# A linear-attention and rational-FFN kernel: another order in its front, chunk 7 by split products, three casts by transfers

## The chip, the cores and the metric

The kernel runs on one core of a Trainium2 chip. The metric is the device time of one launch in microseconds (us), here the median of three runs. A profiled execution has its own time, which is given beside its span (first to last instruction in the trace). Engines: PE (TensorE, matmuls), ACT (ScalarE), DVE (VectorE), POOL (GpSimd), SP (SyncE, which issues most transfers).

## The reference

```
kv  = einsum('bhsd,bhse->bhde', k, v)            # 8 batches, 8 heads, 576 tokens, 64 wide
out = einsum('bhsd,bhde->bhse', q, kv)
x   = out / sqrt(mean(out*out, -1) + 1e-6) * g_norm       # -> 4608 tokens x 512
h   = x @ w_in                                            # 512 x 2048
P   = a0 + a1*h + a2*h^2 + a3*h^3
Q   = 1 + |b0|*|h| + |b1|*h^2
y   = (P / (Q + 1e-6)) @ w_out                            # 2048 x 512
```

The weights come as 64-bit floats and are converted to 32 bits on the chip.

## The kernel before, in words

Tokens go in nine tiles (t) of 512. In each tile the hidden width goes in 16 chunks (c) of 128. One pair (t, c) is a slot; slots run in order (i = 16 t + c). A slot evaluates the rational function of one h (128 x 512 in PSUM) on ACT and DVE (`ew_a` to `ew_d`); PE meanwhile makes the h of the next slot (`gemm1`) and adds the slot two back to the output sums (`gemm2`, tiles `acc`), and it does the attention of the next tile: `kvp` (k times v, from the transferred `kvm`), `op` (kv times q, from `qr`), `ms` (mean squares). All engines follow the order of the code.

Products have two forms. *f32*: one matmul call on 32-bit floats, which the trace shows as two matmuls. *Split*: each operand is a high part (a cast to float32r) and a low part (the rest); three matmuls (high x low, low x high, high x high). Tile 0 uses f32 for `gemm2`, and for `gemm1` of chunks c < `EARLY` (8); later chunks of tile 0 and all other tiles are split. So split parts of tile 0's x and of the weights are needed from chunk 8 on, in `x[0]` and `whl`.

Weights come in units of two chunks, ("wi", c) of w_in and ("wo", c) of w_out. `fetch_w` loads the raw 64-bit words; `signed` (ACT), `lowbits` (ACT or DVE), `conv_b1` and `conv_add` (DVE) make 32-bit floats of them; `split_w` makes the high part with a cast on ACT, and `low_by_transfer`, in the next slot, writes the negated high part on POOL and then issues a transfer from POOL that adds the original on top of it (an accumulating transfer). A dependency puts that negation beside the slot's `q`. `split_x0` does the same for tile 0's x, in two groups of 512 KB. The table `schedule` gives for each unit the slot of the fetch (None and -1: in the front), of the conversion, of the split, and the tags of the SBUF cells for raw words, floats and split parts.

The front (lines 671 to 733) makes tile 0's attention in two halves of 256 tokens: `first_kv`; `first_o(p, k)` for pair p of heads and half k (`op`, half 0 reads `first_qa`, half 1 `first_qb`); `first_squares`; `first_ms` (32 small matmuls); `first_newton` (reciprocal root r: three steps on ACT, two on DVE); `first_rb` (32 small matmuls that spread r); `first_norm` (DVE, four of them, which finish x0). Beside that, unit u0 = ("wi", 0) is converted chunk by chunk (`one`, `two`), then u1 = ("wi", 2) and u2 = ("wo", 0). h of chunks 0 and 1 is made in halves, first half 0 of both, then half 1.

Transfers from SP run through one queue, in the order of their issue; those from POOL through another, on the same 16 transfer engines.

Of the kernel before, what the change touches and what calls it, by code (L numbers as in the profile page):

```python
# [23 lines left out]
def linear_attention_then_rational_ffn(  # L24
# [106 lines left out]
    def f32(t):  # L131
# [3 lines left out]


    schedule = {
# [16 lines left out]
    }  # L154
    units = list(schedule)

# [8 lines left out]
    for c in range(4, NF, 2):  # L165
        made[schedule["wi", c][1] + 1].append(("wi", c, None))

    EARLY = 8
    ON_VECTOR = (("wi", 6),)

    def unsplit(t, c):
# [7 lines left out]
    def fetch_w(u, halves=(slice(0, 2),)):  # L179
        kind, c = u  # L180
        if u not in raws:
            raws[u] = wpool.tile([P, 2 * DM], I64, tag=schedule[u][3], name=f"raw_{kind}{c}")
        src = w_in[c:c + 2].rearrange("c p k f -> p c (k f)") if kind == "wi" else \
            w_out[c:c + 2].rearrange("c p f -> p c f")
        to = raws[u].rearrange("p (c f) -> p c f", c=2)
        for js in halves:
            nc.sync.dma_start(to[:, js], src[:, js])
# [40 lines left out]
    def split_w(u):  # L228
        kind, c = u
        w = ups.pop(u)  # L230
        cells = schedule[u][5]
        if isinstance(cells, str):
            hl = wpool.tile([P, 2, 2 * DM], F32R, tag=cells, name=f"{kind}hl{c}")
            wh, wl = hl[:, 0], hl[:, 1]
        else:
            wh, wl = (wpool.tile([P, 2 * DM], F32R, tag=g, name=f"{kind}{n}{c}") for g, n in zip(cells, "hl"))
        for j in range(2):
            js = slice(j * DM, (j + 1) * DM)
            whl[kind, c + j] = wh[:, js], wl[:, js]
        ACT.copy(wh, w)  # L240
        lows.append((wl, wh, w))

    lows = []
# [6 lines left out]
    def split_x0(g):  # L250
        pool, tag = ((xpool, "xA"), (wpool, "e"))[g]
        xt = pool.tile([P, 2, 2, TW], F32R, tag=tag, name=f"x_0_{g}")
        of = x0[:, 2 * g:2 * g + 2]
        ACT.copy(xt[:, :, 0], of)
        x.setdefault(0, []).extend((xt[:, p, 0], xt[:, p, 1]) for p in range(2))
        lows.append((xt[:, :, 1], xt[:, :, 0], of))

# [373 lines left out]
    def first_o(p, k):  # L631
        q = (qa0, tq0[:, 4 * P:])[k][:, p * HW:(p + 1) * HW]
        PE.matmul(o0[p][k], kvf[:, 0, p], q, start=True, stop=True)

    def first_squares(g, k, made=0):
        for p in range(2 * g + made, 2 * g + 2):
            first_o(p, k)
        for p in range(2 * g, 2 * g + 2):
            ACT.activation(sq0[p][:, halves[k]], o0[p][k], AF.Square)

# [9 lines left out]
    def first_newton(k):  # L650
        cs = slice(k * BW, (k + 1) * BW)
        return newton_rstd(ms0[:, cs], r0[:, cs], r2[:, cs])
# [3 lines left out]
    def first_rb(k):  # L656
        rb0[:] = [oo[p % 2][p // 2][:, 0] for p in range(NPAIR)]
        if k == 0:
            for p, (pool, tag, bufs) in ((1, (ps_at, "at", 1)), (3, (ps_h, "h", 2))):
                rb0[p] = pool.tile([P, TW], F32, tag=tag, name=f"rb_0_{p}", bufs=bufs)[:, 0:HW]  # L660
        for b in range(NBLK):
            for p in range(NPAIR):
                ps = slice(p * Q4, (p + 1) * Q4)
                PE.matmul(rb0[p][:, b * BW:(b + 1) * BW], spread[ps, b], r0[ps, k * BW:(k + 1) * BW], start=True, stop=True)
# [4 lines left out]
            DVE.scalar_tensor_tensor(xp, xp, ghalf, rb0[p], ALU.mult, ALU.mult)  # L669

    u0, u1, u2 = units[:3]
    fetch_w(u0, (one_chunk,))
    nc.sync.dma_start(tq0[:, 4 * P:], of_qb)
    fetch_w(u0, (next_chunk,))
    fetch_w(u1, (one_chunk, next_chunk))
    fetch_w(u2)
    ctx.enter_context(tc.manual_schedule())
# [3 lines left out]
    for p in range(NPAIR):  # L681
        first_kv(p)
        if p < NPAIR - 1:
            warm(1, idle)
    for g in range(2):
        first_squares(g, 0)
        for p in range(2 * g, 2 * g + 2):
            DVE.tensor_copy(x0[:, p, halves[0]], o0[p][0])
# [5 lines left out]
        fetch_w(u)  # L694
    ms0 = ps_at.tile([P, TW], F32, tag="ms", name="ms_0", bufs=1)
    first_ms(0)
    signed(u0, one)
    lowbits(u0, one, "V")
    conv_b1(u0, one)
    newton = first_newton(0)  # L700
    newton()
    conv_add(u0, one)
    first_squares(0, 1)
    signed(u0, two)
    first_o(2, 1)
    first_rb(0)
    first_squares(1, 1, 1)
    lowbits(u0, two)
    first_norm(0)
    h0 = [h_room(0, c) for c in range(2)]  # L710
    gemm1_part(0, 0, h0[0], halves[0], range(0, 2), halves[0])
    first_ms(1)
    gemm1_part(0, 0, h0[0], halves[0], range(2, NPAIR), halves[0])
    conv_b1(u0, two)
    conv_add(u0, two)
    newton = first_newton(1)
    newton()
    for p in range(NPAIR):
        ACT.copy(x0[:, p, halves[1]], o0[p][1])
    ACT.activation(b1abs, abg[:, 5:6], AF.Abs)  # L720
    gemm1_part(0, 1, h0[1], halves[0], range(0, 2), halves[0])
    first_rb(1)
    gemm1_part(0, 1, h0[1], halves[0], range(2, NPAIR), halves[0])
    lowbits(u1, both, "V")
    first_norm(1)
    for c in range(2):
        gemm1_part(0, c, h0[c], halves[1], on=halves[1])
    signed(u1)
    conv_b1(u1, both)
    conv_add(u1, one)  # L730
# [8 lines left out]
    for i, (t, c) in enumerate(slots[:-1]):  # L739
# [17 lines left out]
                evacuate(slots[i - LAG][0])  # L757
        for u in at_slot(2, i):
            split_w(u)
        if i in (1, 3):  # L760
            split_x0(i // 3)
        if i == 0:
            ph = h0[1]
        elif i in (1, 3):
# [78 lines left out]
```

## Time and profile before

| | |
|---|---|
| median of 3 runs | 885.57 us (885.53 to 885.66) |
| profiled execution, own time | 885.92 us |
| its span | 884.2 us |
| PE, DVE, ACT, POOL busy | 876.4, 765.6, 690.1, 87.0 us |
| moved by transfers | 75.10 MB, of it 64.63 by SP's queue, 9.44 by POOL's |

Busy time is that in which an engine has an instruction in work. Matmuls overlap and their ends are modelled, so durations of PE's rows add up to more than the time they take; the distance of two starts is the safer reading. A small wait in square brackets names what ended it.

### The profile page before, as it was taken

The page shows a single profiled execution, that of the slowest core. Times are in us where ns is not written, and L with a number is a line of the kernel's source. Part 1 is how long each engine was busy: PE and PEld are TensorE (multiplying, and loading weights), DVE is VectorE, ACT ScalarE, POOL GpSimd, SP SyncE. Part 2 cuts the span into 40 slices and gives each one's busy share as a digit, 9 for nine tenths or more (in the row PEclk, how much of TensorE's full clock was granted, in tenths as well). Part 3 has the DMA queues.
Part 4 walks back from the last instruction along what each step waited for, and adds up shares of the span by engine and source line. Part 5 has one row for each costly group of instructions (what it writes and reads, how often), then busy time and mean ns, then how long its engine had stood idle before and what let it go on. Part 6 is the DMA issues. An engine that isn't in the chain of part 4 may idle for free.

```text
span 884.2 us, 12008 instructions
## 1 busy us (share of the span) xinstructions
PE 876.4 (99%) x4432; PEld 688.8 (78%) x4432; DVE 765.6 (87%) x1225; ACT 690.1 (78%) x1167; POOL 87.0 (10%) x88
## 2 busy tenths in 40 slices
PE   8999999999999999999999999999999999999998
PEld 6545657878887888888887888788878887888886
DVE  3988898879987998889888997799879988898887
ACT  4999979887877788777877787768767886777665
POOL 3254436422000000000000000000000000000000
PEclk9999999999999999999999999999999999999999
DMA  9987338544122203130223022221002020201001
GB/s 365 393 265 226 72 72 215 140 111 96 60 84 72 49 12 125 35 93 1 72 84 101 8 71 73 73 49 57 27 13 50 9 66 10 49 1 48 0 1 49
DMA packets 26811, 75.10 MB, mean 85 GB/s; under 512 B 2624, under 2 KB 2624, under 8 KB 26752
## 3 DMA queue, kind: packets, MB, share of 16 engines
q1 hardware_dynamic: 23760, 64.63, 21.4%
q0 software_dynamic: 2848, 9.44, 5.9%
q8 instruction: 35, 0.57, 0.3%
q10 hardware_dynamic: 144, 0.26, 0.1%
q14 instruction: 24, 0.20, 0.1%
HBM read 55.32 MB, written 9.57 MB: 73 GB/s over the span
## 4 chain that ended last, share of the span: by engine, by line
PE 94%; DVE 3%; DMA 2%; ACT 1%; issue 0%
PE h L485 14%; PE h L486 13%; PE h L487 13%; PE acc L553 12%; PE acc L555 12%; PE acc L554 12%; PE acc L544 6%; PE h L481 3%; PE kvp L330 2%; DMA first_qb<-in_first_dram 2%; PE ms L404 1%; PE op L387 1%; PE op L388 1%; PE op L386 1%; DVE gl L532 1%; PE op L382 0%
## 5 line engine op out<-in xcount | busy, mean ns | idle before, releaser
L495 ACT ACTIVATE d<-h 128x512 f32<-128x512 f32 x143 | 85.7, 599 | 146.2 <-PE h L487 145.2
L497 DVE SCALAR_TENSOR_TENSOR q<-d,b1abs,q 128x512 f32<-128x512 f32 x143 | 107.1, 749 | 90.6 <-ACT q L496 90.4
L485 PE MATMUL h<-x,wihl 128*128 128x512 f32 (+1 forms) x420 | 167.0, 398 | 0.0
L486 PE MATMUL h<-x,wihl 128*128 128x512 f32 (+1 forms) x420 | 162.8, 388 | 0.0
L487 PE MATMUL h<-x,wihl 128*128 128x512 f32 (+1 forms) x420 | 162.7, 387 | 0.0
L553 PE MATMUL acc<-woh,gl 128*128 128x512 f32 x316 | 123.1, 389 | 0.1
L554 PE MATMUL acc<-wol,gh 128*128 128x512 f32 x316 | 123.0, 389 | 0.0
L555 PE MATMUL acc<-woh,gh 128*128 128x512 f32 x316 | 122.9, 389 | 0.0
L508 ACT ACTIVATE d<-q,bias 128x512 f32<-128x512 f32 x143 | 105.3, 736 | 15.8 <-DVE q L497 15.0
L498 ACT ACTIVATE u<-h,na 128x512 f32<-128x512 f32 x143 | 111.9, 783 | 0.0
L509 ACT ACTIVATE d<-d,bias 128x512 f32<-128x512 f32 x143 | 103.6, 725 | 4.7
L505 DVE SCALAR_TENSOR_TENSOR u<-u,na,h 128x512 f32<-128x512 f32 x143 | 106.1, 742 | 0.6
L515 DVE SCALAR_TENSOR_TENSOR u<-u,na,d 128x512 f32<-128x512 f32 x143 | 106.6, 746 | 0.0
L513 DVE SCALAR_TENSOR_TENSOR q<-q,d 128x512 f32<-128x512 f32 x143 | 98.4, 688 | 0.2 <-ACT d L509 0.2
L499 DVE TENSOR_TENSOR u<-u,h 128x512 f32<-128x512 f32 x143 | 97.8, 684 | 0.4
L496 ACT ACTIVATE q<-h,abg 128x512 f32<-128x512 f32 x143 | 97.9, 685 | 0.0
L485 PEld LDWEIGHTS h<-x,wihl 128*128 128x128 f32 x420 | 78.9, 188 | 23.6 <-DVE q L513 4.2
L486 PEld LDWEIGHTS h<-x,wihl 128*128 128x128 f32 x420 | 78.9, 188 | 16.8 <-issue 1.6
L487 PEld LDWEIGHTS h<-x,wihl 128*128 128x128 f32 x420 | 78.9, 188 | 16.5
L532 DVE TENSOR_TENSOR gl<-u,gh 128x512 fp32r<-128x512 f32 x127 | 90.7, 714 | 0.0
L521 DVE SCALAR_TENSOR_TENSOR u<-q,u 128x512 f32<-128x512 f32 x127 | 87.4, 689 | 2.4
L531 ACT CAST gh<-u 128x512 fp32r<-128x512 f32 x127 | 79.9, 629 | 3.5 <-DVE u L521 3.3
(162 smaller groups left out, 1448.3 us busy)
## 6 DMA issues: line engine op xcount, KB each, us to landing
kvm<-in_kv_dram SPq DMA_DIRECT2D x28, 640.0 KB
raw_wo<-in_w_out_dram SPq DMA_DIRECT2D x8, 1024.0 KB
qr<-in_qT_dram SPq DMA_DIRECT2D x32, 256.0 KB
out_dram<-ob SPq DMA_DIRECT2D x16, 512.0 KB
rb<-rd SPq DMA_DIRECT2D x28, 256.0 KB
raw_wi<-in_w_in_dram SPq DMA_DIRECT2D x6, 1024.0 KB
wihl<-wiw POOLq DMA_DIRECT2D x6, 512.0 KB, 4.5
wol<-wow POOLq DMA_DIRECT2D x5, 512.0 KB, 6.9
```

Source lines behind the costliest of these rows:

```text
L485: PE.matmul(ph, wh, xl, start=(kc == 0), stop=False)
L486: PE.matmul(ph, wl, xh, start=False, stop=False)
L487: PE.matmul(ph, wh, xh, start=False, stop=(kc == NPAIR - 1))
L497: q_made = DVE.scalar_tensor_tensor(q, d, b1abs, q, ALU.mult, ALU.add)
L498: ACT.activation(u, ph, AF.Identity, bias=na[:, 2:3], scale=na[:, 3:4])
L505: DVE.scalar_tensor_tensor(u, u, na[:, 1:2], ph, ALU.add, ALU.mult)
L508: ACT.activation(d, q, AF.Ln, bias=bias[:, 2:3], scale=QSC)
L509: ACT.activation(d, d, AF.Exp, bias=bias[:, 3:4], scale=-1.0)
L515: DVE.scalar_tensor_tensor(u, u, na[:, 0:1], d, ALU.add, ALU.mult)
L553: PE.matmul(o, gl[:, ss], wh, start=(c == 0), stop=False)
L554: PE.matmul(o, gh[:, ss], wl, start=False, stop=False)
L555: PE.matmul(o, gh[:, ss], wh, start=False, stop=(c == NF - 1))
```

## The change

- Front, transfers: `first_qb` is issued ahead of both chunks of u0, where it stood between them.
- Front, order: all four `first_o` of half 1 run directly behind `first_ms(0)`, where they stood in two pieces behind the first conversion. Newton of half 0 comes ahead of u0's conversion; `first_ms(1)` ahead of h_0's first half, which is no longer cut in two; the copies of x (ACT) ahead of `first_newton(1)`; `first_rb(1)` ahead of h_1's first half; the low bits of u1 behind `first_norm(1)`.
- `EARLY` is 7: h of chunk 7 in tile 0 is made by split products. For this ("wi", 6) is split in slot 3, where it was split in slot 17, and its low part follows in slot 4.
- The high parts of tile 0's x (both groups, slot 0; before, slots 1 and 3) and of ("wi", 6) are made by transfers from POOL that convert on the way, where ACT cast them. The low parts of x follow in slots 2 and 3 (before, 2 and 4).
- The table: other cells for split parts, and later fetches of four units.

```diff
     schedule = {
-        ("wi", 0): (None, None, 11, "g0", "f0", "g3"),
-        ("wi", 2): (None, None, 13, "g1", "f1", "g5"),
+        ("wi", 0): (None, None, 11, "g0", "f0", ("f4", "f6")),
+        ("wi", 2): (None, None, 13, "g1", "f1", ("f8", "f10")),
...
-        ("wi", 6): (-1, 1, 17, "g4", "f4", ("f10", "f12")),
+        ("wi", 6): (-1, 1, 3, "g4", "f4", "g4"),
...
-        ("wi", 14): (3, 8, 10, "g4", "f12", "g4"),
-        ("wo", 10): (4, 9, 23, "g5", "f13", ("f5", "f4")),
-        ("wo", 12): (6, 11, 25, "g7", "f14", ("f7", "f9")),
-        ("wo", 14): (8, 13, 27, "g1", "f15", ("f11", "f13")),
+        ("wi", 14): (4, 8, 10, "g5", "f12", "g5"),
+        ("wo", 10): (6, 9, 23, "g7", "f13", ("f3", "f5")),
+        ("wo", 12): (8, 11, 25, "g1", "f14", ("f7", "f9")),
+        ("wo", 14): (10, 13, 27, "g3", "f15", ("f11", "f13")),
...
-    EARLY = 8
+    EARLY = 7
+    CAST_ON_THE_WAY = (("wi", 6),)
...
-        ACT.copy(wh, w)
+        if u in CAST_ON_THE_WAY:
+            POOL.dma_start(wh, w)
+        else:
+            ACT.copy(wh, w)
...
-        ACT.copy(xt[:, :, 0], of)
+        POOL.dma_start(xt[:, :, 0], of)
         x.setdefault(0, []).extend((xt[:, p, 0], xt[:, p, 1]) for p in range(2))
-        lows.append((xt[:, :, 1], xt[:, :, 0], of))
+        return xt[:, :, 1], xt[:, :, 0], of
...
-    fetch_w(u0, (one_chunk,))
     nc.sync.dma_start(tq0[:, 4 * P:], of_qb)
-    fetch_w(u0, (next_chunk,))
+    fetch_w(u0, (one_chunk, next_chunk))
...
     first_ms(0)
-    signed(u0, one)
-    lowbits(u0, one, "V")
-    conv_b1(u0, one)
+    for p in range(NPAIR):
+        first_o(p, 1)
     newton = first_newton(0)
     newton()
+    first_squares(0, 1)
+    lowbits(u0, one, "V")
+    signed(u0, one)
+    first_rb(0)
+    first_squares(1, 1)
+    first_ms(1)
+    conv_b1(u0, one)
     conv_add(u0, one)
-    first_squares(0, 1)
-    signed(u0, two)
-    first_o(2, 1)
-    first_rb(0)
-    first_squares(1, 1, 1)
-    lowbits(u0, two)
     first_norm(0)
     h0 = [h_room(0, c) for c in range(2)]
-    gemm1_part(0, 0, h0[0], halves[0], range(0, 2), halves[0])
-    first_ms(1)
-    gemm1_part(0, 0, h0[0], halves[0], range(2, NPAIR), halves[0])
+    gemm1_part(0, 0, h0[0], halves[0], on=halves[0])
+    for p in range(NPAIR):
+        ACT.copy(x0[:, p, halves[1]], o0[p][1])
+    newton = first_newton(1)
+    newton()
+    signed(u0, two)
+    lowbits(u0, two)
+    first_rb(1)
     conv_b1(u0, two)
     conv_add(u0, two)
...
-        if i in (1, 3):
-            split_x0(i // 3)
+        if i == 0:
+            x0_lows = [split_x0(g) for g in range(2)]
+        if i in (1, 2):
+            lows.append(x0_lows[i // 2])
```

PE in the front, before, behind the first sums of squares (`op_1_0`, `op_1_1`: half 1 of the heads' pairs; `op_0_0` with L664: the spread r; `ms`: the second sums of squares; the left-out rows repeat the spread, or the sums, for other heads and blocks):

```order
L633 MATMUL op_1_0_155<-first_qb,kvf 128x256 x2
L633 MATMUL op_1_1_156<-first_qb,kvf 128x256
L664 MATMUL op_0_0_153<-r_162,spread 128x64
...
L633 MATMUL op_1_1_156<-first_qb,kvf 128x256
L481 MATMUL h_0_322<-x_161,wiw_282 128x256 x2
L648 MATMUL ms_263<-sq_0_157,sels 32x64
...
L481 MATMUL h_0_322<-x_161,wiw_282 128x256 x2
L481 MATMUL h_1_323<-x_161,wiw_282 128x256 x2
L664 MATMUL op_0_0_153<-r_162,spread 128x64
...
L481 MATMUL h_1_323<-x_161,wiw_282 128x256 x2
L481 MATMUL h_0_322<-x_161,wiw_282 128x256 x4
L481 MATMUL h_1_323<-x_161,wiw_282 128x256 x4
```

The same place after the change (lines of the changed file, two to four higher):

```order
L637 MATMUL op_1_0_155<-first_qb,kvf 128x256 x2
L637 MATMUL op_1_1_156<-first_qb,kvf 128x256 x2
L666 MATMUL op_0_0_153<-r_162,spread 128x64
...
L650 MATMUL ms_263<-sq_0_157,sels 32x64
...
L485 MATMUL h_0_336<-x_161,wiw_329 128x256 x4
L666 MATMUL op_0_0_153<-r_162,spread 128x64
...
L485 MATMUL h_1_337<-x_161,wiw_329 128x256 x4
L485 MATMUL h_0_336<-x_161,wiw_329 128x256 x4
L485 MATMUL h_1_337<-x_161,wiw_329 128x256 x4
```

The second sums of squares and the second spread now each stand ahead of products of h that they stood behind, or in the middle of.

POOL behind the front, before (`kvh`, `kvl`: the small operations of pairs 0 and 1; `x_0`, `x_1`: the two groups of tile 0's split x; TENSOR_SCALAR on them is the negation, the DMA behind it the accumulating transfer; `wihl_593` is unit ("wi", 8)):

```order
L270 TENSOR_TENSOR kvl_138<-kvf,kvh_132 64x64
L246 TENSOR_SCALAR x_0_434<-x_0_434 128x2x512
L247 DMA x_0_434<-x_161 128x2x512
L269 TENSOR_SCALAR kvh_133<-kvf 64x64
L270 TENSOR_TENSOR kvl_139<-kvf,kvh_133 64x64
L269 TENSOR_SCALAR kvh_133<-kvf 64x64
L270 TENSOR_TENSOR kvl_139<-kvf,kvh_133 64x64
L246 TENSOR_SCALAR x_1_540<-x_1_540 128x2x512
L247 DMA x_1_540<-x_161 128x2x512
L246 TENSOR_SCALAR wihl_593<-wihl_593 128x1024
L247 DMA wihl_593<-wiw_522 128x1024
```

And after the change, where L258 and L242 are the converting transfers, the first two standing ahead of pair 0's small operations, and `wihl_544` is ("wi", 6):

```order
L258 DMA x_0_409<-x_161 128x2x512
L258 DMA x_1_411<-x_161 128x2x512
...
L250 TENSOR_SCALAR x_0_409<-x_0_409 128x2x512
L251 DMA x_0_409<-x_161 128x2x512
L250 TENSOR_SCALAR x_1_411<-x_1_411 128x2x512
L251 DMA x_1_411<-x_161 128x2x512
L242 DMA wihl_544<-wiw_471 128x1024
L273 TENSOR_SCALAR kvh_133<-kvf 64x64
...
L250 TENSOR_SCALAR wihl_544<-wihl_544 128x1024
L251 DMA wihl_544<-wiw_471 128x1024
L250 TENSOR_SCALAR wihl_595<-wihl_595 128x1024
```

Pair 1's small operations now stand behind x's second negation and two more issues, and the negation of ("wi", 6) stands behind them.

## Rows read from the trace of the kernel before

Columns of a timeline row: start in us, length in us (of all its instructions together), engine, line, operation, tile written <- tiles read, count, and in brackets the engine's idle time before it and what ended it. ACTq, SPq and the like are an engine's queue.

**Rows 1.** The page: PE's busy time, and the granted TensorE clock in 40 equal slices of the span (9 is 90% or more).

```profile
PE 876.4 (99%) x4432; PEld 688.8 (78%) x4432; DVE 765.6 (87%) x1225; ACT 690.1 (78%) x1167; POOL 87.0 (10%) x88
...
PEclk9999999999999999999999999999999999999999
```

**Rows 2.** Waits of PE over the whole span: who waited for whom, us in total, times, longest (the first of five rows; the others are 1.0 or less).

```profile
PE op L633 <- DMA first_qb<-in_first_dram: 1.3, 1, 1.3
...
```

**Rows 3.** Timeline of PE in the front.

```profile
12.20 0.91 PE L648 MATMUL ms<-sq,sels 128*32 128x64 f32 x28 [0.24 <-ACT sq L639]
14.41 1.56 PE L633 MATMUL op<-first_qb,kvf 128*128 128x256 f32 x6 [1.30 <-DMA first_qb<-in_first_dram]
15.90 0.32 PE L664 MATMUL op<-r,spread 32*128 32x64 f32 x1
...
17.66 1.13 PE L481 MATMUL h<-x,wiw 128*128 128x256 f32 x4
18.72 0.65 PE L648 MATMUL ms<-sq,sels 128*32 128x64 f32 x32
...
21.23 1.43 PE L664 MATMUL op<-r,spread 32*128 32x64 f32 x32
22.59 8.02 PE L481 MATMUL h<-x,wiw 128*128 128x256 f32 x28
24.64 5.97 PE L481 MATMUL h<-x,wiw 128*128 128x256 f32 x19
```

**Rows 4.** Timeline of ACT in the front (L284: newton's last step on ACT; L639: squares; L202: `signed`).

```profile
13.99 0.26 ACT L284 ACTIVATE r<-r 128x64 f32<-128x64 f32 x1
15.58 0.66 ACT L639 ACTIVATE sq<-op 128x256 f32<-128x256 f32 x2 [1.33 <-PE op L633]
16.12 0.66 ACT L202 ACTIVATE raw_wi<-raw_wi 128x512 f32<-128x512 f32 x1
17.69 0.66 ACT L639 ACTIVATE sq<-op 128x256 f32<-128x256 f32 x2 [0.91 <-PE op L633]
...
19.45 0.31 ACT L282 ACTIVATE r<-ms,bias 128x64 f32<-128x64 f32 x1 [0.53 <-PE ms L648]
...
20.17 0.26 ACT L284 ACTIVATE r<-r 128x64 f32<-128x64 f32 x1
```

**Rows 5.** Timeline of DVE in the front (L288: newton's last step; L669: the norm, four of them; L220 and L224: shift and add of the conversion).

```profile
14.54 0.23 DVE L288 SCALAR_TENSOR_TENSOR r<-r,r 128x64 f32<-128x64 f32 x1
...
17.13 0.48 DVE L669 SCALAR_TENSOR_TENSOR x<-x,ghalf,op 128x256 f32<-128x256 f32 x1 [1.76 <-PE rb L664]
...
18.31 0.48 DVE L669 SCALAR_TENSOR_TENSOR x<-x,ghalf,rb 128x256 f32<-128x256 f32 x1
18.70 0.42 DVE L220 TENSOR_SCALAR wiw<-raw_wi 128x512 int32<-128x512 int32 x1
19.25 0.69 DVE L224 CUSTOM_DVE_ANT_0 wiw<-raw_wi,wiw 128x1024 uint16<-128x1024 uint16 x1
...
20.72 0.22 DVE L288 SCALAR_TENSOR_TENSOR r<-r,r 128x64 f32<-128x64 f32 x1
```

**Rows 6.** Transfer queues: packets, MB moved, time as a share of 16 engines; first row SP's queue from 0 to 11.6 us, second row the queue that fetches instructions from 11.2 to 12.4 us.

```profile
q1 hardware_dynamic: 1089, 3.48, 79.3%
...
q8 instruction: 1, 0.02, 5.7%
```

**Rows 7.** Timeline of PE around h of chunk 7 (between the first two rows) and of chunk 9 (between the last two).

```profile
66.33 1.14 PE L382 MATMUL op<-qr,kvf 128*128 128x64 f32 x4
67.31 3.60 PE L481 MATMUL h<-x,wiw 128*128 128x512 f32 x8
70.74 0.59 PE L544 MATMUL acc<-wow,g 128*128 128x512 f32 x1
...
81.29 1.14 PE L382 MATMUL op<-qr,kvf 128*128 128x64 f32 x4
...
85.01 0.59 PE L544 MATMUL acc<-wow,g 128*128 128x512 f32 x1
```

**Rows 8.** SP's queue from 0 to 41 us; PE's products of pair 1; POOL's queue from 47 to 50 us and from 60 to 63 us; time from issue to landing of the two accumulating transfers of x, and of six of units of w_in.

```profile
q1 hardware_dynamic: 4211, 15.23, 94.9%
...
46.17 0.80 PE L330 MATMUL kvp<-kvm 128*64 128x64 f32 x20
...
q0 software_dynamic: 231, 0.47, 105.2%
...
q0 software_dynamic: 256, 0.50, 95.0%
...
DMA to landing us min/median/max: 5.5/6.2/6.8
...
DMA to landing us min/median/max: 4.5/4.5/4.9
```

**Rows 9.** Timeline around slot 3 and 5: DVE's q of slot 3, and POOL's small operations and negation.

```profile
47.00 0.75 DVE L497 SCALAR_TENSOR_TENSOR q<-d,b1abs,q 128x512 f32<-128x512 f32 x1
...
50.41 0.82 POOL L269 TENSOR_SCALAR kvh<-kvf 64x64 fp32r<-64x64 f32 x1 [4.39 <-ACT kvf L267]
...
54.93 2.77 POOL L246 TENSOR_SCALAR x<-x 128x1024 fp32r<-128x1024 f32 x1 [0.81 <-DVE q L497]
...
66.00 2.14 POOL L269 TENSOR_SCALAR kvh<-kvf 64x64 fp32r<-64x64 f32 x1
...
68.98 0.37 POOL L269 TENSOR_SCALAR kvh<-kvf 64x64 fp32r<-64x64 f32 x1
```

More of the change, by code (lines that the diff above doesn't have):

```diff
@@ L633, in first_o, with first_squares @@
         PE.matmul(o0[p][k], kvf[:, 0, p], q, start=True, stop=True)
-    def first_squares(g, k, made=0):
-        for p in range(2 * g + made, 2 * g + 2):
-            first_o(p, k)
+    def first_squares(g, k):
         for p in range(2 * g, 2 * g + 2):
@@ L685, in linear_attention_then_rational_ffn @@
     for g in range(2):
+        for p in range(2 * g, 2 * g + 2):
+            first_o(p, 0)
         first_squares(g, 0)
@@ L696, in linear_attention_then_rational_ffn @@
     first_ms(0)
-    signed(u0, one)
-    lowbits(u0, one, "V")
-    conv_b1(u0, one)
+    for p in range(NPAIR):
+        first_o(p, 1)
     newton = first_newton(0)
     newton()
-    conv_add(u0, one)
-    first_squares(0, 1)
-    signed(u0, two)
-    first_o(2, 1)
-    first_rb(0)
-    first_squares(1, 1, 1)
-    lowbits(u0, two)
+    first_squares(0, 1)
[5 more added lines that the diff above has]
+    conv_b1(u0, one)
+    conv_add(u0, one)
     first_norm(0)
     h0 = [h_room(0, c) for c in range(2)]
-    gemm1_part(0, 0, h0[0], halves[0], range(0, 2), halves[0])
-    first_ms(1)
-    gemm1_part(0, 0, h0[0], halves[0], range(2, NPAIR), halves[0])
+    gemm1_part(0, 0, h0[0], halves[0], on=halves[0])
[6 more added lines that the diff above has]
+    first_rb(1)
     conv_b1(u0, two)
     conv_add(u0, two)
[L716 to L719, printed above, removed]
     ACT.activation(b1abs, abg[:, 5:6], AF.Abs)
[L721 to L724, printed above, removed]
+    gemm1_part(0, 1, h0[1], halves[0], on=halves[0])
     first_norm(1)
@@ L727, in linear_attention_then_rational_ffn @@
         gemm1_part(0, c, h0[c], halves[1], on=halves[1])
+    lowbits(u1, both, "V")
     signed(u1)
```

6 rows, old and new, of the table schedule are left out of this document.

## The prediction

> **What bounds the kernel now.** I first read the page's busy shares: PE works 99% of the span, with the granted clock at 9 tenths or more in all 40 slices [rows 1]. Next, whom PE waited for: the only wait of weight is 1.3 us in the front, for `first_qb` [rows 2]. So the time is PE's work, plus the front's idle time, plus any wait that the change adds. ACT and DVE are busy but trail PE; what they save counts for nothing unless PE waits for it. Then PE's timeline of the front [rows 3]: behind the first sums of squares (12.20, 0.91 long) PE stands until 14.41. After that it passes from one dependent piece to the next until 22.59, where 28 matmuls run back to back: four of h_1's first half, sixteen of both second halves, eight of h_2. From there on PE has work all the time, so what the front gains by then is what the kernel gains, if nothing later waits.
>
> **Part 1, the front: order alone.** `first_qb` becomes the eighth transfer and u0's first chunk the ninth. By 11.6 us the load queue had moved 3.48 MB [rows 6] and the first eight transfers are 3.15 MB, so the eighth has landed by then. A ninth, 0.52 MB at about 0.41 MB a us, is due at 12.9; PE's wait for the ninth ended at 14.41, 1.5 later. The fetch queue's row explains that: 5.7% of 16 engines over 1.2 us is 1.1 us on a single engine [rows 6], and a transfer is done when its slowest engine is. So qb is there by 11.6, and the late one is now u0's first chunk, at 14.4.
>
> I replay the front with the durations of before [rows 3 to 5].
> - PE: the four `first_o` of half 1 start behind ms(0), at 13.0 instead of 14.41, and take 1.7 to 1.8.
> - ACT: newton's last step ends at 14.25 as before. Squares of half 1 follow PE's start by 1.17 (14.41 to 15.58 before), so 14.25 too; `signed` 0.54 later, 14.8 to 15.5 (its load landed at 14.4: no wait); the other squares 15.4 to 16.0.
> - PE: the first spread starts 0.3 behind r (20.94 to 21.23 before; r is at 14.77), at 15.1, and serves the norm 1.23 later (15.90 to 17.13 before), 16.3. ms(1) starts 0.37 behind the squares (18.35 to 18.72 before), 16.4 to 17.05.
> - DVE: low bits, the shift behind `signed` at 15.55, the add 0.55 later (18.70 to 19.25 before), 16.1, the norm some 0.6 behind that: 16.7 instead of 17.13. The conversion, not the spread, now decides here.
> - PE: h_0's first half 17.2 to 19.0. Newton(1) on ACT 17.1 to 18.1, on DVE behind the fourth norm 18.3 to 18.75, so the second spread starts at 19.05 instead of 21.23, and the next product 1.36 later as before (21.23 to 22.59): 20.4. u0's second half, some 0.7 an operation on ACT and DVE from 18.1, is ready at 20.1, hidden by that spread.
>
> From 20.4 it is 24 matmuls to h_2, before 20 from 22.59, each 0.22 (nine between 22.59 and 24.64): 22.59 + 4.4 - 20.4 - 5.3 = **1.3 us earlier**. Bounds: 0.4 if only the norm's start counts (17.13 to 16.7), 1.4 if PE's whole first wait does (14.41 to 13.0).
>
> **Part 2, chunk 7.** Four f32 products (eight rows of the trace) become twelve split ones. Both forms stand in the trace between the same neighbours: from the start of `op` to that of `acc` it is 66.33 to 70.74 with chunk 7, and 81.29 to 85.01 with chunk 9, which is split already [rows 7]. 4.41 - 3.72 = **0.69 us off**. PE waits for nothing there, so it counts in full while the operands are in time.
>
> **Part 3, the converting transfers.** Three casts leave ACT: nothing, as no wait of PE ends on them [rows 2]; a gain from them is excluded. They become POOL transfers of 512 KB. Two are issued when x is normed, at 21 to 24 us, into a train of loads: by 41 us the load queue moved 15.23 MB [rows 8], and everything up to `kvm` of pair 1 adds up to 15.21 MB. Its last bytes are due at 40.9, and with the engine that is 1.5 late at 42.4 (an estimate). What the two casts take of the 16 engines, 2c, pushes that back. PE needs `kvm` 1 at 46.17 [rows 8], now 1.3 earlier, 44.85. The wait is 42.4 + 2c - 44.85, about 2c - 2.4.
>
> No row shows a converting transfer. Below: 1.28 us, 512 KB at the train's rate. Above: an accumulating one, 0.50 MB in 3 us at 95% of the engines, so 3.0, or with the 47 to 50 row 3.4 [rows 8]. An accumulate reads two operands for each one that it writes, a cast one, so the lower row is nearer; I take 1.33, and the wait is **0.25 us**. `kvm` of pair 0 (8.0 MB into the train, due at 24) is needed behind h_2, at 29: it holds up to c = 2.5.
>
> The Trainium skill speaks against 1.33: its page "DMA: Bandwidth & Descriptors", section "Bandwidth", has 6.15 us of busy time for 1 MB through GpSimd's queue. Half of that, an estimate of 3.1 us for a cast, would make the wait 3.8 and the sum 887.3. The accumulates here agree with that size; no run shows a cast.
>
> The third cast stands on POOL behind the second negation of x and ahead of pair 1's four small operations. The chain to chunk 7's low parts, 1.05 earlier than before: q of slot 3 at 46.7, negation 46.85 to 49.6, its transfer issued at 49.9 and the cast by 52.1, small operations 3.7 (50.41 to 54.12) until 55.8 [rows 9]. The cast ends about 1.3 behind x's accumulate, which lands 5.5 to 6.8 from its issue: 56.7 to 58. Negation 2.77, 0.3 to the issue, 4.5 to 4.9 to land [rows 8]: 64.3 to 66.0. h_7's second product wants it at about 66.5 (67.31 is h_7's start before). Nothing, with little cover; every us later would be PE's.
>
> **Part 4, the table.** Fetches moved later by one or two slots still have three slots of some 7 us (67.31 to 81.92 is two [rows 7]) for a 1 MB load of 2.6; the new cells hold finished tiles. Nothing; a late fetch would show as ACT waiting in `signed`.
>
> **Sum**, against the profiled execution's 885.92 (span 884.2, 1.7 around it): -1.3 + 0.25 - 0.69 = -1.74, so 884.2. That execution is 0.35 above the median of the three runs: 885.57 - 1.74 = **883.8 us**. Part 3's wait caps the front: a larger gain there only makes PE wait longer for `kvm` 1.
>
> **Rivals.**
> - *`kvm` 1 on time*: the late engine does not recur, or casts go below 1.2. -2.0, 883.55. For it: the delay came from one fetch. Against: the program up to there is the same.
> - *Casts cost what accumulates cost* (the slower side): at c = 3.4 PE waits 4.4 ahead of `kvp` of pair 1, and -2.0 + 4.4 = +2.4 gives 888.0. No change at c = 2.2, slower by 0.2% from c = 3.1; at 2.8 it is 886.8. For it: same queue, same sizes, and from 47 to 50 the accumulate left the loads next to nothing. Against: the second operand.
> - *h_7 late*: the negation of `wi` 6 starts when its cast lands, no longer beside h. Beside DVE's conversions a POOL operation of 0.37 took 2.14 [rows 9]; 1.8 more gives 67.8, a wait of 1.3: 885.1. The Trainium skill, page "SBUF — State Buffer", section "Who interferes with whom", has DVE and GpSimd shut each other out for whole instructions; the trace agrees in kind, with 2.14 against 0.37. Against it: 2.77 for a negation beside h.
> - *The front gives little*, 0.4: `kvm` 1 is then on time, and -1.1 makes 884.5.
>
> **How the numbers follow.** 0.2% (1.77 us) is about what a measurement of this kernel can tell from no change; faster is below 883.8, slower above 887.3. Likeliest, 0.47, with its own range of 883.5 to 884.2: a little under half of it on the faster side (0.22). `kvm` 1 on time, 0.20: faster. Casts dear, 0.15: 0.09 slower, the rest same. h_7 late, 0.10, and little front, 0.08: same. Faster 0.42, same 0.49, slower 0.09. The range leaves out the dear half of the casts and the very best front: 883.2 to 886.5.
>
> **What would show it.** Right: no wait of PE for `first_qb`; h_2's first product near 25.7 instead of 27.0; chunk 7's twelve products in 2.8 us; a PE wait of some tenths ahead of `kvp` of pair 1. Wrong: more than 2 us of engine time for a cast; PE waiting for a transfer inside h_7; PE idle before h_0's products by half a us more than replayed, with DVE's conversion behind it.

## The result and the profile after

| | before | after |
|---|---|---|
| median | 885.62 us (885.53 to 885.89) | 891.46 us (890.12 to 891.55) |
| ratio to before, 95% interval | | 1.0061 (1.0048 to 1.0074) |
| span of the profiled execution | 884.2 us | 889.6 us |

The forecast was 883.8 us, a gain of 1.7; measured is a loss of 5.8. The granted clock on the page of after, to be held against [rows 1]:

```profile
PEclk9998999999999999999999999999999999999999
```

PE is as full as before (99% of the span), but one slice of the granted clock, the fourth (67 to 89 us), is below 9. The longest wait of PE over the whole span, to be held against [rows 2]:

```profile
PE h L490 <- DMA wihl<-wiw: 4.4, 1, 4.4
```

The front's wait for `first_qb` is gone, and a new one of 4.4 us stands there, for the transfer that completes the low part of ("wi", 6) (`wihl`). PE's timeline in the front [rows 3] and at the first load-bound products [rows 8]:

```profile
13.01 1.99 PE L637 MATMUL op<-first_qb,kvf 128*128 128x256 f32 x8
...
17.05 1.99 PE L485 MATMUL h<-x,wiw 128*128 128x256 f32 x8 [0.40 <-DVE x L671]
18.97 1.12 PE L666 MATMUL op<-r,spread 32*128 32x64 f32 x32
20.02 8.88 PE L485 MATMUL h<-x,wiw 128*128 128x256 f32 x32
28.83 0.80 PE L334 MATMUL kvp<-kvm 128*64 128x64 f32 x20
...
45.04 0.80 PE L334 MATMUL kvp<-kvm 128*64 128x64 f32 x20 [0.50 <-ACT q L500]
```

`kvp` of pair 0 stood at 30.54 before: the front is 1.71 earlier. At `kvp` of pair 1 (46.17 before) 1.13 is left. The releaser named there, ACT's q, is not what PE waits for: in the kernel with the front alone (below) `kvp` of pair 1 starts at 44.41, before that q ends (45.23). Where the third cast is on ACT again (below too), the same gap is put down to the transfer of `kvm`:

```profile
PE kvp L334 <- DMA kvm<-in_kv_dram: 0.7, 1, 0.7
```

`kvm` comes later because the load queue lost room to x's casts. From 0 to 41 us of the changed kernel it moved [rows 8]:

```profile
q1 hardware_dynamic: 3983, 14.35, 89.6%
```

That is 0.88 MB less than the 15.23 of before.

And PE around h of chunk 7 [rows 7] in the changed kernel:

```profile
64.95 1.14 PE L386 MATMUL op<-qr,kvf 128*128 128x64 f32 x4
65.57 0.74 PE L489 MATMUL h<-x,wihl 128*128 128x512 f32 x1
70.72 0.77 PE L490 MATMUL h<-x,wihl 128*128 128x512 f32 x1 [4.40 <-DMA wihl<-wiw]
71.28 0.63 PE L491 MATMUL h<-x,wihl 128*128 128x512 f32 x1
71.71 0.63 PE L489 MATMUL h<-x,wihl 128*128 128x512 f32 x1
...
75.55 4.27 PE L548 MATMUL acc<-wow,g 128*128 128x512 f32 x8
79.75 0.80 PE L334 MATMUL kvp<-kvm 128*64 128x64 f32 x20
```

The second product starts 5.15 us behind the first. In chunk 9 of the kernel before, which stands behind an `op` too and waits for nothing, that distance is 0.57:

```profile
81.92 0.74 PE L485 MATMUL h<-x,wihl 128*128 128x512 f32 x1
82.49 0.39 PE L486 MATMUL h<-x,wihl 128*128 128x512 f32 x1
```

So PE stood for 4.58. Then the products follow each other at 0.43 instead of 0.23. The granted clock says why (columns: window, PE busy and instructions, granted clock, DMA share, GB/s):

```profile
65.00:70.00 5.00, 1.32 (x6) 1.00 0.72 109
70.00:71.00 1.00, 0.28 (x1) 0.54 1.10 383
71.00:72.00 1.00, 1.00 (x3) 0.50 0.97 385
...
76.00:77.00 1.00, 1.00 (x2) 0.55 1.06 291
77.00:78.00 1.00, 1.00 (x4) 1.00 1.03 254
```

PE had stood since 66.3; at 70 the granted clock fell from 2.4 to 1.2 GHz (1.00 to 0.50) and came back at 77, some 6 us after PE took up work. The Trainium skill, page "TensorE: Matmul & The Clock Gate", section "What's actually happening", has these two levels set by how busy PE has been; the trace agrees. From `op` to `acc` it is 10.60 instead of the 3.72 of a split chunk, and from `acc` to `kvp` 4.20 instead of 3.53: 7.55 lost, 4.58 by the wait and 2.97 by the clock.

Why the low part came late stands in POOL's timeline [rows 8, 9]:

```profile
42.62 1.27 POOL L251 DMA_DIRECT2D x<-x  x1 [0.31 <-POOL x L250]
...
48.97 1.24 POOL L251 DMA_DIRECT2D x<-x  x1 [0.30 <-POOL x L250]
49.73 1.07 POOL L242 DMA_DIRECT2D wihl<-wiw  x1
...
61.70 3.11 POOL L250 TENSOR_SCALAR wihl<-wihl 128x1024 fp32r<-128x1024 f32 x1 [8.46 <-DVE wow L225]
65.11 0.91 POOL L251 DMA_DIRECT2D wihl<-wiw  x1 [0.30 <-POOL wihl L250]
```

Of the transfers issued from 45 to 62 us these are POOL's (the last column is the time from issue to landing):

```profile
x<-x POOLq DMA_DIRECT2D x1, 512.0 KB, 9.5
wihl<-wiw POOLq DMA_DIRECT2D x1, 512.0 KB, 11.4
```

The cast (L242) is issued earlier than I had replayed, but lands 11.4 us later, at 61.2; the negation can only start then, though POOL has been idle for 8.5 us. (The releaser named there, DVE's L225, ended at 61.57; it can account for 0.5 at most.) Ahead of these two transfers stood x's first accumulating transfer: issued at 42.62, it had its first packets at 47.1 and landed only after 11.7 us, at 54.3.

### The profile page after: what moved, and what is told of

Read it like the earlier page. It is cut to its first block, busy times and chain, and to the rows that moved or that the text cites. A ratio compares the mean times of both kernels' runs of the same rounds, so it can differ in the third digit from the quotient of the medians.

```text
span 889.6 us, 12021 instructions
## 1 busy us (share of the span) xinstructions
PE 878.5 (99%) x4436; PEld 691.9 (78%) x4436; DVE 767.6 (86%) x1225; ACT 687.5 (77%) x1164; POOL 87.2 (10%) x91
## 4 chain that ended last, share of the span: by engine, by line
PE 88%; DVE 6%; ACT 2%; DMA 1%; issue 1%; POOL 0%; SPq 0%; ACTq 0%; POOLq 0%
PE h L489 14%; PE h L490 13%; PE h L491 13%; PE acc L557 12%; PE acc L559 12%; PE acc L558 12%; PE acc L548 4%; PE kvp L334 2%; PE ms L408 1%; PE op L391 1%; PE op L392 1%; DVE u L509 1%; DVE u L503 1%; DMA first_g<-in_first_dram 1%; PE op L390 1%
## 5 line engine op out<-in xcount | busy, mean ns | idle before, releaser
L490 PE MATMUL h<-x,wihl 128*128 128x512 f32 (+1 forms) x360 | 140.6, 390 | 4.4 <-DMA wihl<-wiw 4.4
L489 PE MATMUL h<-x,wihl 128*128 128x512 f32 (+1 forms) x360 | 144.2, 401 | 0.0
L491 PE MATMUL h<-x,wihl 128*128 128x512 f32 (+1 forms) x360 | 140.3, 390 | 0.0
L512 ACT ACTIVATE d<-q,bias 128x512 f32<-128x512 f32 x143 | 105.2, 736 | 16.0 <-DVE q L501 14.4
L557 PE MATMUL acc<-wohl,gl 128*128 128x512 f32 x256 | 99.6, 389 | 0.0
L558 PE MATMUL acc<-wohl,gh 128*128 128x512 f32 x256 | 99.6, 389 | 0.0
L559 PE MATMUL acc<-wohl,gh 128*128 128x512 f32 x256 | 99.6, 389 | 0.0
L557 PE MATMUL acc<-woh,gl 128*128 128x512 f32 x252 | 98.2, 390 | 0.1
L558 PE MATMUL acc<-wol,gh 128*128 128x512 f32 x252 | 98.1, 389 | 0.0
L559 PE MATMUL acc<-woh,gh 128*128 128x512 f32 x252 | 98.0, 389 | 0.0
L489 PEld LDWEIGHTS h<-x,wihl 128*128 128x128 f32 x360 | 68.1, 189 | 21.5 <-DVE q L517 4.2
```

What stands on the lines that cost most here:

```text
L489: PE.matmul(ph, wh, xl, start=(kc == 0), stop=False)
L490: PE.matmul(ph, wl, xh, start=False, stop=False)
L491: PE.matmul(ph, wh, xh, start=False, stop=(kc == NPAIR - 1))
L512: ACT.activation(d, q, AF.Ln, bias=bias[:, 2:3], scale=QSC)
L557: PE.matmul(o, gl[:, ss], wh, start=(c == 0), stop=False)
L558: PE.matmul(o, gh[:, ss], wl, start=False, stop=False)
```

## The experiments

Medians and ratios are against runs of the kernel before on the same chip (885.7 to 885.8). Positions are starts of PE's rows, less those of before.

**Front alone.** The table is that of before too; against the changed kernel:

```diff
...
-    EARLY = 7
-    CAST_ON_THE_WAY = (("wi", 6),)
+    EARLY = 8
+    CAST_ON_THE_WAY = ()
...
-        POOL.dma_start(xt[:, :, 0], of)
+        ACT.copy(xt[:, :, 0], of)
...
-        if i == 0:
-            x0_lows = [split_x0(g) for g in range(2)]
-        if i in (1, 2):
-            lows.append(x0_lows[i // 2])
+        if i in (1, 3):
+            split_x0(i // 3)
```

> The front's new order and `first_qb` as eighth transfer, all else as before: chunk 7 f32, casts on ACT, the table of before. My theory (the front is worth what its trace after the change shows, 28.83 against 30.54 at the first products of the next tile, and the loss stands in h_7 alone): 1.7 us off, 883.9, no wait of PE ahead of pair 1's `kvp`, since the two casts of x no longer stand in the load train. The forecast's own size, 1.3: 884.3. Rival (the new order costs something later that the trace after the change hides behind h_7): 885.6 or more.

Measured: 884.65, ratio 0.9984 (0.9975 to 0.9992). `kvp` of pairs 0 to 3 stand 1.77, 1.76, 1.74 and 1.75 earlier, without a wait between 20 and 80 us. In the trace 1.71 holds up to the last sums of squares at 748 us; 0.24 is lost behind them, near the end, whose cause is open, and the span is 1.5 shorter (882.7). The median shows 1.15, but its interval, 0.7 to 2.2, takes 1.7 in. So up to the last tile the new front costs nothing later.

**The third cast by ACT again.**

```diff
-    CAST_ON_THE_WAY = (("wi", 6),)
+    CAST_ON_THE_WAY = ()
```

> The changed kernel, only the high part of (wi, 6) is cast by ACT in slot 3 again (about 1.0 us, at 47 to 48), x's two casts stay transfers. My theory (the third converting transfer waits on POOL's queue until 61.2, and with it the negation and the low part until 70.6): the negation can start beside q of slot 4 at about 54, the low part lands at 62 to 63, h_7 does not wait, the clock stays at 1.00. Sum: -1.7 + 0.6 (kvp of pair 1) - 0.7 = -1.8, 883.8. Rival (the accumulating transfers and negations are slow in this stretch whoever makes the high part): PE still waits in h_7, 1 us or more, 885 to 888.

Measured: 884.04, ratio 0.9979 (0.9970 to 0.9988); clock 1.00, no wait in h_7. POOL's timeline has the negation of ("wi", 6):

```profile
53.53 2.77 POOL L250 TENSOR_SCALAR wihl<-wihl 128x1024 fp32r<-128x1024 f32 x1
```

The negation starts 8.2 earlier than with the transfer. One cast of about 1 us moved back to ACT is worth 7.4 us: the loss hangs on the third cast.

**Work for PE in the wait.** The added products are overwritten.

```diff
+            if (t, c, kc) == (0, 7, 0):
+                for _ in range(21):
+                    PE.matmul(ph, wh, xl, start=True, stop=True)
             PE.matmul(ph, wh, xl, start=(kc == 0), stop=False)
```

> The changed kernel with 21 more products of h_7's first kind ahead of its first (same operands, into the same bank, overwritten): PE has 4.8 us of work while the low part is on its way. My theory (7.5 us are lost around h_7: 4.9 by the wait, 2.6 by a granted clock of 0.50 from 70 to 77 that follows on PE's idle time): h_7's second product still starts at about 70.7, but the clock stays at 1.00 and the twelve products and the eight behind them take 2.8 and 3.5 us: 2.6 off the changed kernel, 888.8. Rival (the clock falls for another reason, the transfers or POOL's and DVE's work of that stretch): it falls here too, 891.4 or a little more.

Measured: 890.76, ratio 1.0055 (1.0042 to 1.0068). The clock stays up, and `kvp` of pair 3 stands at 77.27 instead of 79.75, 2.48 earlier. The window from 70 to 75 us (columns as above):

```profile
70.00:75.00 5.00, 5.00 (x21) 1.00 0.99 330
```

And PE's timeline, with h_7's second product, `kvp` of pair 3 and h_8's second product (h's lines are three higher in this file):

```profile
71.25 0.39 PE L493 MATMUL h<-x,wihl 128*128 128x512 f32 x1
...
77.27 0.80 PE L334 MATMUL kvp<-kvm 128*64 128x64 f32 x20
79.86 0.50 PE L493 MATMUL h<-x,wihl 128*128 128x512 f32 x1 [1.37 <-DMA wihl<-wiw]
```

From h_7's second product to `kvp` of pair 3 it is 6.02 here and 9.03 in the changed kernel (70.72 to 79.75): the slow clock costs 3.0. The 4.9 and 2.6 of my expectation were a wrong split of the 7.5, with 0.23 for the first distance where 0.57 is right; that 2.48 came so near to 2.6 is luck, as this kernel's h_7 stands 0.3 later and its second product half a us later. Most of the 2.48 is given back at h_8, which waits 1.37. So the clock's share of 3.0 us is shown, and that the next unit, ("wi", 8), is late as well: its negation stands behind that of ("wi", 6) on POOL. The slow clock had hidden that.

**Chunk 7 by f32 again**, with ("wi", 6) split as in the changed kernel.

```diff
-    EARLY = 7
+    EARLY = 8
```

> The changed kernel, but h of chunk 7 by f32 products again, so (wi, 6)'s split parts are made as early as in the changed kernel and nobody in tile 0 waits for them. My theory: the front's 1.7 less the 0.6 ahead of kvp of pair 1, -1.1, 884.5, clock 1.00 throughout. Rival (the transfers and the negations on POOL slow DVE down, q of slot 5 took 1.52 instead of 0.75, and PE waits for DVE or for loads somewhere else): 885.5 or more, with waits of PE between 60 and 80 us.

Measured: 892.43, ratio 1.0071 (1.0059 to 1.0083). My expectation was wrong by 8 us. PE's longest wait:

```profile
PE h L490 <- DMA wihl<-wiw: 5.3, 1, 5.3
```

POOL's negation of ("wi", 8), and the window behind the wait:

```profile
66.10 3.06 POOL L250 TENSOR_SCALAR wihl<-wihl 128x1024 fp32r<-128x1024 f32 x1
```
```profile
80.00:85.00 5.00, 5.00 (x12) 0.50 0.60 116
```

Nobody waits for ("wi", 6) now, and yet the damage is larger: its late negation holds that of ("wi", 8) back on POOL until 66.10 (62.30 before), and h_8 waits at 79.48, again with half the clock behind it. What waits in POOL's order counts, not only what PE asks for.

**x's casts by ACT**, in slots 1 and 2, the third by a transfer.

```diff
-        POOL.dma_start(xt[:, :, 0], of)
+        ACT.copy(xt[:, :, 0], of)
...
-        if i == 0:
-            x0_lows = [split_x0(g) for g in range(2)]
         if i in (1, 2):
-            lows.append(x0_lows[i // 2])
+            lows.append(split_x0(i // 2))
```

> The changed kernel with x's two casts on ACT (slots 1 and 2; the low parts stay in slots 2 and 3); only (wi, 6) is cast by a transfer. Theory A (x's casts, 3.2 us of the 16 engines, push the train of loads into 47 to 52, where before it had ended; there the loads take half of the engines from x's accumulating transfers, and the third cast stands behind them): without them the train is over by 47, x's low parts land by 51 and 54 to 55, the cast by 57, (wi, 6)'s low part by 65 to 66; PE waits neither ahead of kvp of pair 1 nor, more than 0.3, in h_7, the clock stays at 1.00: -1.75 - 0.69, 883.2 to 883.5. Theory B (the cast is late by its place behind x's two accumulating transfers and beside loads, whatever stood ahead of them): the cast lands at 59 or later, PE waits 2 us or more in h_7: 886 to 890.

Measured: 895.87, ratio 1.0105 (1.0085 to 1.0126). The runs spread from 891.05 to 897.59. Theory A falls: without x's casts h_7 waits 10.5 us, which is more than theory B had as well. POOL's timeline, with the second accumulating transfer of x, the cast, and the negation behind it:

```profile
50.56 1.25 POOL L251 DMA_DIRECT2D x<-x  x1 [0.31 <-POOL x L250]
51.36 1.05 POOL L242 DMA_DIRECT2D wihl<-wiw  x1
63.57 2.91 POOL L250 TENSOR_SCALAR wihl<-wihl 128x1024 fp32r<-128x1024 f32 x1 [8.63 <-DMA wihl<-wiw]
```

From 52 to 56 us, after x's second accumulating transfer had been issued, the queues moved:

```profile
q1 hardware_dynamic: 355, 1.16, 95.4%
q0 software_dynamic: 7, 0.01, 1.2%
```

POOL's queue (q0) got next to nothing while the load queue (q1) was full: 4 us pass between the end of the issue (51.8) and its packets (55.8), and it lands 11.6 behind its issue, the cast 12.0. The low part behind them meets loads too: issued at 66.78, it is there for PE at 76.98, 10.2 later, where the changed kernel has 5.6.

**Loads out of the way.**

```diff
-        ("wi", 12): (2, 6, 8, "g2", "f10", "g2"),
-        ("wo", 8): (2, 7, 21, "g3", "f11", ("f1", "f2")),
-        ("wi", 14): (4, 8, 10, "g5", "f12", "g5"),
+        ("wi", 12): (5, 6, 8, "g2", "f10", "g2"),
+        ("wo", 8): (5, 7, 21, "g3", "f11", ("f1", "f2")),
+        ("wi", 14): (6, 8, 10, "g5", "f12", "g5"),
```

> The changed kernel with three loads of 1 MB fetched later: (wi, 12) and (wo, 8) in slot 5 instead of 2, (wi, 14) in slot 6 instead of 4; POOL's order untouched. If the third cast is late because POOL's transfers start late and get half of the engines beside a busy load queue: the load train ends 5 us earlier, at about 42, x's first accumulating transfer starts within 1 us of its issue (44.5 instead of 47.1), the cast lands at 55.5 to 57.5 instead of 61.2, (wi, 6)'s low part at 63 to 65.5; no wait in h_7, clock 1.00: -1.75 + 0.7 - 0.69, 883.9 to 884.2. If the place behind two accumulating transfers is the whole cause: the cast still lands 9 us or more behind its issue, 59 or later, and 2 us or more of h_7's wait stay: 887 to 891.

Measured: 884.55, ratio 0.9988 (0.9980 to 0.9997). The two queues from 46 to 48 us in this kernel:

```profile
q0 software_dynamic: 177, 0.34, 97.3%
q1 hardware_dynamic: 8, 0.03, 3.8%
```

The same from 48 to 51 us in the changed kernel:

```profile
q0 software_dynamic: 147, 0.30, 54.0%
q1 hardware_dynamic: 146, 0.58, 51.6%
```

And POOL's negation of ("wi", 6) in this kernel:

```profile
59.13 2.77 POOL L250 TENSOR_SCALAR wihl<-wihl 128x1024 fp32r<-128x1024 f32 x1 [5.37 <-DMA wihl<-wiw]
```

x's first accumulating transfer has its packets at 45.0, 0.6 behind the end of its issue (3.2 in the changed kernel), and lands after 6.5 us (11.7); the cast takes 8.4 instead of 11.4. The wait in h_7 is 0.45 instead of 4.4 and the clock stays up: the loads are most of the cause. The cast still lands 1 us later than I gave for that theory; that the accumulating transfer ahead of it accounts for the rest is argued, not shown. The time is 0.35 above the forecast's upper end: from `kvp` of pair 3 to the next `kvp` it is 59.02, where 58.64 before, and the cause of that is open.

**The cast ahead of x's second group in POOL's order.**

```diff
         q_made = ew_a(t, c, ph)
+        held = []
+        if i == 3:
+            x_low = lows.pop()
+            split_w(("wi", 6))
+            held.append(lows.pop())
+            lows.append(x_low)
         for todo in lows:
...
-        lows.clear()
+        lows[:] = held
...
         for u in at_slot(2, i):
-            split_w(u)
+            if i != 3:
+                split_w(u)
```

> The changed kernel with one swap in POOL's order: the third cast is issued ahead of the negation and the accumulating transfer of x's second group, where it stood behind them. Theory B (its place behind x's accumulating transfers makes it late): it lands some 3 to 4 us earlier, at 57 to 58, (wi, 6)'s low part at about 66, at most 1 us of wait in h_7, clock 1.00: 884 to 885. Theory A (the loads that share the engines from 47 to 58 make it late): it lands at 59 or later and 2 us or more of the wait stay, with the fall of the clock: 888 to 891.

Measured: 884.03, ratio 0.9979 (0.9970 to 0.9988). POOL's cast and the negation that waits for it:

```profile
45.28 0.58 POOL L242 DMA_DIRECT2D wihl<-wiw  x1 [1.25 <-DVE wiw L221]
...
56.31 2.79 POOL L250 TENSOR_SCALAR wihl<-wihl 128x1024 fp32r<-128x1024 f32 x1 [2.86 <-DMA wihl<-wiw]
```

The cast lands no faster (10.9 us from its issue) but is issued 4.45 earlier, and that is enough: no wait in h_7. So neither theory was clean. How long a transfer of POOL takes depends on the loads, when it is issued depends on POOL's order, and a change of either alone cures most of it.

**No converting transfer.** The edits of the two ACT experiments together.

> The changed kernel with no converting transfer: x's high parts by ACT in slots 1 and 2, (wi, 6)'s in slot 3; the front and chunk 7 as changed. Both theories: no wait ahead of kvp of pair 1, none in h_7, clock 1.00: the front 1.75 and chunk 7 0.69, 883.2; against the front alone 0.7 less, which is the price of chunk 7's f32 form. Rival (ACT's three casts of 1.0 us stand in PE's way in slots 1 to 3, as these transfers were meant to avoid): waits of PE for ACT or DVE between 30 and 55 us of some tenths each, 883.8 or more.

Measured: 885.02, ratio 0.9989 (0.9981 to 0.9998). The rival held, with more than I gave it. PE's longest wait behind the start, and then ACT's timeline ahead of it:

```profile
PE op L386 <- ACT kvf L271: 1.0, 1, 1.0
```

```profile
48.55 1.03 ACT L244 CAST wihl<-wiw 128x1024 fp32r<-128x1024 f32 x1
49.49 0.43 ACT L271 COPY kvf<-kvp 64x64 f32<-64x64 f32 x2
```

The third cast stands ahead of the copy of pair 1's `kvf`, for which PE's `op` waits: 0.96 lost against the kernel before. ACT's timeline of the kernel before has the same in small, with x's second cast there:

```profile
49.17 1.03 ACT L254 CAST x<-x 128x1024 fp32r<-128x1024 f32 x1
50.10 0.43 ACT L267 COPY kvf<-kvp 64x64 f32<-64x64 f32 x2
```

From `kvp` of pair 1 to that of pair 2 it is 12.46 before, 12.20 in the changed kernel: 0.25 gained by a cast that I had priced at nothing.

**Only x's casts by transfers.** The first kernel has the table of before:

```diff
+        ("wi", 6): (-1, 1, 17, "g4", "f4", ("f10", "f12")),
...
+        ("wi", 14): (3, 8, 10, "g4", "f12", "g4"),
...
+    EARLY = 8
+    CAST_ON_THE_WAY = ()
```

The second has the changed table but for one row:

```diff
-        ("wi", 6): (-1, 1, 3, "g4", "f4", "g4"),
+        ("wi", 6): (-1, 1, 9, "g4", "f4", "g4"),
...
+    EARLY = 8
+    CAST_ON_THE_WAY = ()
```

> The front's new order with x's two casts by transfers, chunk 7 f32, (wi, 6) and the table as before. Mine: the front's 1.75 less the wait ahead of kvp of pair 1, 0.7, and no other wait of PE, since x's low parts (landing at 54 and 58 to 59) have time until h_8 at about 72: 884.7 to 885.3, the same as or 0.7 above the front alone. Rival (the later low parts of x push (wi, 8)'s low part past h_8, at 72): PE waits there 1 us or more, 886 or more.

> The kernel with only x's casts by transfers (front as changed, chunk 7 f32, (wi, 6) cast by ACT), once more, now with the changed table, in which (wi, 14) is fetched in slot 4 instead of 3 and into another cell, so that no load stands ahead of pair 2's kvm and waits for a cell; (wi, 6) is split in slot 9. If the 2.8 us ahead of kvp of pair 2 came from the old table's order of loads: that wait goes, 0.7 ahead of pair 1 stays, -1.75 + 0.75: 884.8. If they came from x's casts and late low parts themselves: the wait stays, 887.5 or more.

Measured: 888.37, ratio 1.0028 (1.0019 to 1.0038), and 886.20, ratio 1.0003 (0.9995 to 1.0012). In the first, PE's waits have:

```profile
PE kvp L334 <- DMA kvm<-in_kv_dram: 3.5, 2, 2.8
```

The timeline of SP's queue shows why:

```profile
44.56 0.37 SPq L188 DMA_DIRECT2D raw_wi<-in_w_in_dram  x1
44.98 0.47 SPq L312 DMA_DIRECT2D kvm<-in_kv_dram  x1
```

The fetch of ("wi", 14) waits for a cell, and `kvm` of pair 2 stands behind it; in the changed kernel that is issued at 39.09. With the new table the 2.8 are gone and 0.8 ahead of pair 1 stay, as forecast; up to 73 us that kernel stands 1.06 ahead. Its time is no gain all the same: from 120 to 134 us PE waits for DVE (0.30 and 0.34 in two rows), and at tile 2's sums of squares it is 0.18 behind (185.24 against 185.06). From `kvp` of pair 3 to the next `kvp` it takes 59.85 there, but 58.65 in the kernel with the third cast by ACT, which has the same table but for that row, and 58.64 before. So the loss came with my split in slot 9 and not with the rest of the table; by what path, no run shows.

**A version of both halves.** The order of the cast-ahead kernel, and of x's casts only the second group's by a transfer:

```diff
-        POOL.dma_start(xt[:, :, 0], of)
+        (POOL.dma_start if g else ACT.copy)(xt[:, :, 0], of)
...
         if i == 0:
-            x0_lows = [split_x0(g) for g in range(2)]
-        if i in (1, 2):
-            lows.append(x0_lows[i // 2])
+            x_low_1 = split_x0(1)
+        if i == 1:
+            lows.append(split_x0(0))
+        if i == 2:
+            lows.append(x_low_1)
```

> A version meant to beat both: front and table as changed, chunk 7 by split products, (wi, 6) cast by a transfer that is issued ahead of x's second accumulating transfer, and of x's two casts only the second group's by a transfer (the first by ACT in slot 1). If the wait ahead of kvp of pair 1 is set by the 1.6 us of 16 engines that each cast takes from the load train: half of it leaves no wait there, and nothing else waits: -1.75 - 0.69, 883.2. Rival (ACT is late in slots 1 to 3 with a cast of 1.0 us in slot 1, or the casts are issued into other company and land late): a wait of PE for ACT's kvf or in h_7, 884 or more.

Measured: 883.39, ratio 0.9973 (0.9963 to 0.9983). It beats both kernels, by 2.4 us the one before. PE has no wait between 20 and 80 us, and in its timeline `kvp` of pair 3 (74.27 before) is 2.20 earlier:

```profile
72.07 0.80 PE L334 MATMUL kvp<-kvm 128*64 128x64 f32 x20
```

The parts are 1.28 from the front, 0.25 and 0.67, as in the sum below. In this execution (883.75) the front gave 0.4 less than in the changed kernel; the median is 0.36 below this execution.

## Why the prediction was wrong, point by point

- **The front: right, 1.71 for 1.3.** No wait for `first_qb`, h_0's first half at 17.05 (17.2 replayed), the second spread at 18.97 (19.05). The spread then hands over after 1.05, where I had taken the 1.36 of before.
- **`kvm` 1: right in kind, 0.57 lost for 0.25.** From 26 to 33 us x's casts moved 0.93 MB in 40% of 7 us, which makes 1.6 us of the 16 engines for each cast (1.33 taken). That is an upper bound, as the load queue's packets count 69.8% beside them, 110% together. What the loads lost says more: the 0.88 MB above are 2.2 us at 0.41 MB a us for both casts, or 1.1 for each. The wait is larger all the same. The front brought 0.4 more, and the sum said that a larger gain there only makes PE wait longer. And `kvm` came 1.9 behind the end of its bytes (an estimate: 40.9 + 2.2 = 43.1 against 45.04), not 1.5. That 1.5 was misread: of the ninth transfer's 0.52 MB 0.33 had moved by 11.6 us (3.48 less 3.15), so it was due at 12.1 and came 2.3 late, and the fetch's 1.1 is half of that. With one cast instead of two (the last version) no wait is left, though in an execution whose front brought only 1.28, so that `kvm` was wanted 0.4 later there. The rival "casts cost what accumulates cost" is refuted for the cast by itself, and with it the estimate of 3.1 us from the Trainium skill (page "DMA: Bandwidth & Descriptors", section "Bandwidth"): a cast took 1.1 to 1.6.
- **Casts off ACT: wrong, 0.25 gained for nothing.** The prediction went by PE's list of waits, whose shown rows name none on ACT; a loss of 0.25, split over two gaps (0.14 ahead of `op`, 0.11 behind it), isn't in it.
- **Chunk 7: right.** From `kvp` of pair 2 to that of pair 3 it is 0.67 less than before in three kernels (third cast by ACT, cast ahead, the last version); 0.69 forecast.
- **The table: nothing, as forecast (58.65 against 58.64 above), but it was needed.** With x's casts as transfers the old order costs 2.8 ahead of `kvp` of pair 2.
- **The third cast: the step that failed.** The prediction has "about 1.3 behind x's accumulate, which lands 5.5 to 6.8 from its issue: 56.7 to 58". Those times came from rows in which POOL's queue had the engines to itself [rows 8], with 95% and 105% of them. In the changed kernel the load queue is still full when POOL's transfers start: x's second accumulating transfer took 9.5, the cast 11.4, landing at 61.2, 3.2 to 4.5 later than forecast. The rest of the chain added some 1.6 to 2.0: 0.5 until the negation starts, negation 3.11 (2.77), then 5.6 from the issue to PE's start (4.5 to 4.9 taken). I had reckoned with the train being pushed back by x's casts for `kvm`, and not asked whom the pushed train meets. The experiments without x's casts and with later loads show that the meeting itself is the price, with x's casts ahead of it or without.
- **Rival "h_7 late": the right place, the wrong size.** It had a wait of 1.3 through a slow negation. DVE and POOL did hold each other up (2.17 for DVE's shift at 65.48, 0.7 elsewhere, beside the negation behind it), but that gave tenths; the wait of 4.58 came from the landing, and 2.97 more from the clock, which no rival had. The prediction's list of what would show it wrong does name PE waiting for a transfer inside h_7.

The sum by the trace: -1.71 + 0.57 - 0.25 - 0.67 + 4.58 + 2.97 = +5.49; PE's last product is 5.49 later than before.

## What to carry to other kernels

A transfer's time from issue to landing belongs to the company in which it was measured: before you put it into a chain, look at what the other queues will be moving when it is issued. A chain of several transfers through a shared queue should be issued as early as its operands allow and not behind work that nobody waits for, since its lateness is handed on to the next unit. And a wait of some us on a TensorE that is otherwise full is dearer than its length: price the slow clock behind it too.

## What the runs showed of the hardware

- Beside a full load queue POOL's first packet came 3.2 us behind the end of the issue (x's first cast and x's first accumulating transfer in the changed kernel), 4.0 and 4.4 in the kernel with x's casts by ACT. With the load queue idle it came after 0.6 (the low part of ("wi", 6) in the changed kernel), and with the later loads after 0.6 too, where the load queue ran dry at that moment. Once both had begun, an accumulating transfer and the loads moved at about half of the engines' time each, 54.0% and 51.6%.
- It went the other way too: in the kernel before, two loads were issued at 46.52 and 46.94, and the load queue had 4.2% of the engines from 47 to 50 us, while x's accumulating transfer had 105.2% [rows 8].
- The granted clock fell from 1.00 to 0.50 after PE had stood for some 4 us, and came back 6 us after it had work again; products of 512 columns then start 0.43 apart instead of 0.23, and 3.0 us were lost by it. In the kernel with work in the wait it stayed at 1.00 in the same place, with the same transfers around it, and so it did where PE stood for 0.45 (later loads).
- A converting transfer of 512 KB (128 partitions, packets of 2048 bytes) took 1.1 us of the 16 engines by what the loads lost, 1.6 by its packets' time; an accumulating one of the same size took 3.0 to 3.5 (0.50 MB in 95.0% and 0.47 MB in 105.2% of 3 us [rows 8]).
